# Routing search and proposals with one of each VectorE step's two operands in PSUM

## The chip, the cores and the metric

One core of one Trainium2 chip runs the whole program. The metric is the device time of one execution in microseconds (us); lower is better.

## What is computed

Three layers run one after the other on 4608 tokens of 512 values, all in float32: a retention layer (causal linear attention with a decay per head), a bilinear layer `((x @ w1) * (x @ w2)) @ w3 @ w_out`, and a mixture of eight experts whose tokens are assigned globally. Only the assignment matters here:

```python
cap = N // E                      # 4608 / 8 = 576
logits = x @ w_gate               # 4608 x 8
order = np.argsort(-logits.flatten())
for idx in order:
    tok, e = (int(idx) // E, int(idx) % E)
    if assigned[tok] >= 0 or counts[e] >= cap:
        continue
    assigned[tok] = e
    counts[e] += 1
for e in range(E):
    mask = assigned == e
    h = np.maximum(x[mask] @ w1[e], 0.0)
    out[mask] = h @ w2[e]
```

## The kernel before, in words

The bilinear layer's last product (`y`, 12 blocks of 384 tokens) is only partly done in its own turn. For eight of the blocks it is put off: 24 tiles of 128 tokens, with 24 matmuls each (L893, 576 in all), are left to fill TensorE while the tokens are assigned. These matmuls are called fillers below. For a filler tile ScalarE makes the high part of its input (L888), GpSimd the low part (L889, a tensor_tensor of 128x1024), and ScalarE copies the result out of PSUM (L896); SyncE stores it to `y_scratch`.

The assignment (`route`) is a search for one threshold per expert. It has five rounds and a last check. A round is:

- `propose`: TensorE broadcasts the thresholds `tau` (L694); VectorE masks the logits `LB` below the threshold (L696, L697), takes each token's best expert (`best`, a tensor_reduce at L668), masks what is not the best (L699, L700); TensorE transposes the proposals (L673) and ScalarE copies them to `LP` (L703).
- `search`: VectorE sets up a table of step widths `hs_` (L709, or L711 to L713) and the first trial thresholds (L714). Then come six trips. In a trip VectorE and ScalarE count proposals above three trial thresholds (L716, L717 on VectorE, L719 on ScalarE), a matmul adds the counts up (L676, called the count below), and VectorE compares them with the capacity (L726), moves the trial thresholds (L725 prepares, L728 sets) and `tau` (L729).

Then `place` turns the chosen tokens into a list of token numbers by expert: the running place of each token is compared with the numbers 0 to 127 (`iota`; VectorE, L768 and four times L774), GpSimd multiplies by token numbers (four times L773), 48 small matmuls (L779) collect them, and VectorE writes `idx` (L785). With `idx` GpSimd gathers the rows of the first expert (L977), and the experts' matmuls begin (L1010, L1032).

Every engine works through its own instructions in the order in which they were written down. `merge(route(), lates, LATE)` sets that order here: each `yield` of the routing code names a time, and for it a matching number of fillers is put behind the routing matmul on TensorE's list. So 11 fillers follow a count (in one pair of trips 12 and 10), 5 follow the last count of a round, and 35 stand between the broadcast L694 and the first count of a round (26 in the first round). In the last check 21 stand between L694 and L673. A routing matmul that is late holds up every filler behind it.

`RS` (which holds `tau`, `thr`, `ahead`, `hits`, `r3`), `A2` (`r1`, `r2`, `LP`, `hs_`), `LB` and the constants `C(...)` are in SBUF. `PX[1]` and the two halves `PYb` of the tile `py` are PSUM banks that the attention and the experts use and that stand idle during the routing.

Of the kernel before, what the change touches and what calls it, by code (L numbers as in the profile page):

```python
# [9 lines left out]
AF = mybir.ActivationFunctionType  # L10
OP = mybir.AluOpType
# [5 lines left out]
PT = 96  # L17
# [3 lines left out]
TRIPS = 8  # L21
# [63 lines left out]
def build(ctx, tc, io):  # L85
    nc = tc.nc
    PE, V, A, G, SP = nc.tensor, nc.vector, nc.scalar, nc.gpsimd, nc.sync
# [10 lines left out]
    def C(name):  # L98
        o, n = COFF[name]
        return cst[:, o:o + n]  # L100
# [3 lines left out]
    def region(tag, n, dt):  # L104
        uid[0] += 1
        return sb.tile([128, n], dt, name=f"{tag}_{uid[0]}", tag=tag)
# [6 lines left out]
    A0, A1, A2 = region("a0", 3072, F32), region("a1", 3072, F32), region("a2", 1536, F32)  # L113
# [7 lines left out]
    TR, PX, MM = P[0:2], P[2:4], P[4:6]  # L121
    PY = ps.tile([128, 1024], F32, name="py")
    PYb = [PY[:, 512 * i:512 * i + 512] for i in range(2)]
# [9 lines left out]
    def nxt(name, n):  # L133
        i = rot[name]
        rot[name] = (i + 1) % n
        return i
# [494 lines left out]
    NEG = -1e38  # L631
# [5 lines left out]
    ts_i, ts_f, r3, rt = RS[:PT, 704:800].bitcast(I32), RS[:PT, 800:896], RS[:PT, 896:944], RS[:, 944:1008]  # L637
    r1, r2, LP = A2[:PT, 0:384], A2[:PT, 384:768], A2[:, 768:1056]
    idx = sb.tile([128, 40], I32, name="idx")
    flag = sb.tile([1, 2], I32, name="flag")  # L640
    w0, w0n, tau, wid, hits, off = (rt[:, i:i + 1] for i in range(6))
    thr, ahead, junk = (rt[:, 8 + 3 * i:11 + 3 * i] for i in range(3))
    hs_ = A2[:, 1056:1056 + 6 * TRIPS]
    sc2 = MS[:, 0:288]
    cnt = rh[:, 0:1]

# [7 lines left out]
    def f3(x):  # L654
        return x.rearrange("p (c n) -> p c n", c=3)

    def bcast_j(x):

        return x.rearrange("p (c j) -> p c j", c=3)[:, :, None, :].to_broadcast([PT, 3, 8, 16])

    def f4(x):
        return x.rearrange("p (c e j) -> p c e j", c=3, e=8)

    LBf = LB.rearrange("p c e j -> p (c e j)")

    def best(m):

        V.tensor_reduce(r3.rearrange("p (c j) -> p c j", c=3), m.rearrange("p (c e j) -> p c j e", c=3, e=8),  # L668
                        axis=AX.X, op=OP.max)

    def to_experts(src, out_ps):
        for c in range(3):
            PE.transpose(out_ps[:, PT * c:PT * c + PT], src[:, 128 * c:128 * c + 128], ident[:PT, :PT])  # L673

    def count(out_ps, x):
        PE.matmul(out_ps, blk16, x, start=True, stop=True)  # L676
# [14 lines left out]
    def propose():  # L691

        p = TR[nxt("tr", 2)]
        PE.matmul(p[:PT, :128], tau.to_broadcast([128, PT]), ident, start=True, stop=True)  # L694
        yield 3700
        V.tensor_tensor(f3(r1), f3(LBf), p[:PT, None, :128].to_broadcast([PT, 3, 128]), op=OP.is_lt)  # L696
        V.scalar_tensor_tensor(r1, r1, NEG, LBf, op0=OP.mult, op1=OP.add)  # L697
        best(r1)
        V.tensor_tensor(f4(r2), f4(r1), bcast_j(r3), op=OP.is_lt)  # L699
        V.scalar_tensor_tensor(r1, r2, NEG, r1, op0=OP.mult, op1=OP.add)  # L700
        p = TR[nxt("tr", 2)]
        to_experts(r1, p)
        A.activation(LP, p[:, :288], AF.Copy)  # L703
        yield 2300

    def search(a, trips):

        if a == 0:
            V.tensor_scalar(hs_, C("pw"), w0, 2.0, op0=OP.mult, op1=OP.mult)  # L709
        else:  # L710
            V.tensor_scalar(wid, tau, w0n, 2.0 - 2.0 ** a, op0=OP.is_equal, op1=OP.mult)  # L711
            V.tensor_scalar(wid, wid, 2.0 ** a, w0, op0=OP.add, op1=OP.mult)
            V.tensor_scalar(hs_, C("pw"), wid, None, op0=OP.mult)  # L713
        V.scalar_tensor_tensor(thr, C("sg"), tau, hs_[:, 0:3], op0=OP.mult, op1=OP.add)  # L714
        for i in range(trips):
            V.tensor_scalar(sc, LP, thr[:, 0:1], 0.0, op0=OP.is_ge, op1=OP.add, accum_out=rh[:, 5:6])  # L716
            V.tensor_scalar(sc, LP, thr[:, 1:2], 0.0, op0=OP.is_ge, op1=OP.add, accum_out=rh[:, 6:7])  # L717
            with nc.allow_low_precision(reason="whole numbers up to 288"):
                A.activation(sc2, LP, AF.Sign, bias=thr[:, 2:3], accum_out=rh[:, 7:8])  # L719
            p = TR[nxt("tr", 2)]  # L720
            count(p[:, :3], rh[:, 5:8])
            last = i == trips - 1
            step = hs_[:, 3 * TRIPS + 3 * i:3 * TRIPS + 3 * i + 3]
            if not last:
                V.scalar_tensor_tensor(ahead, C("sg"), tau, hs_[:, 3 * i + 3:3 * i + 6], op0=OP.mult, op1=OP.add)  # L725
            V.scalar_tensor_tensor(junk, p[:, :3], 0.0, C("cap"), op0=OP.add, op1=OP.is_ge, accum_out=hits)  # L726
            if not last:
                V.scalar_tensor_tensor(thr, step, hits, ahead, op0=OP.mult, op1=OP.add)  # L728
            V.scalar_tensor_tensor(tau, step[:, 0:1], hits, tau, op0=OP.mult, op1=OP.add)  # L729
            yield 900 if last else 1900  # L730

    def final_check():
# [13 lines left out]
    def place():  # L746

        V.tensor_tensor_scan(sc, sel, sel, 0.0, op0=OP.add, op1=OP.bypass)
        p = TR[nxt("tr", 2)]
        PE.matmul(p[:, :1], tri16, cnt, start=True, stop=True)  # L750
        yield 1500
        V.tensor_tensor(off, p[:, :1], C("ebase"), op=OP.add)
        V.scalar_tensor_tensor(sc, sc, off, sel, op0=OP.add, op1=OP.mult)
        p = TR[nxt("tr", 2)]
        for c in range(3):
            PE.transpose(p[:PT, 128 * c:128 * c + 128], sc[:, PT * c:PT * c + PT], ident)  # L756
        yield 2000
        V.tensor_reduce(r3.rearrange("p (c j) -> p c j", c=3), p[:PT, :384].rearrange("p (c e j) -> p c j e", c=3, e=8),
                        axis=AX.X, op=OP.max)
        V.tensor_scalar(ts_i[:, 0:48], r3, -1.0, None, op0=OP.add)  # L760
        V.tensor_scalar(ts_i[:, 48:96], ts_i[:, 0:48], 7, None, op0=OP.logical_shift_right)
        V.tensor_scalar(ts_i[:, 0:48], ts_i[:, 0:48], 127, None, op0=OP.bitwise_and)
        V.tensor_copy(ts_f, ts_i)
        pi = PX[0]
        o1, ot = (x[:PT, 3072:4032].bitcast(F16).rearrange("p (n s) -> p n s", s=40) for x in spare[:2])
        lo = gt[NB - 3][:PT].bitcast(F16).rearrange("p (n s) -> p n s", s=128)

        V.tensor_tensor(o1, C("iota")[:PT, None, :40].to_broadcast([PT, 48, 40]),  # L768
                        ts_f[:, 48:96, None].to_broadcast([PT, 48, 40]), op=OP.is_equal)
        yield 2000  # L770
        for a in range(0, 48, 12):
            b = a + 12
            G.tensor_tensor(ot[:, a:b], o1[:, a:b], C("tok")[:PT, a:b, None].to_broadcast([PT, 12, 40]), op=OP.mult)  # L773
            V.tensor_tensor(lo[:, a:b], C("iota")[:PT, None, :].to_broadcast([PT, 12, 128]),  # L774
                            ts_f[:, a:b, None].to_broadcast([PT, 12, 128]), op=OP.is_equal)
            yield 1700
        for ch in range(48):
            g = ch // 16
            PE.matmul(pi[:, 40 * g:40 * g + 40], lo[:, ch], ot[:, ch], start=ch == 0, stop=ch % 16 == 15,  # L779
                      skip_group_check=True)  # L780
        yield 1000
        V.scalar_tensor_tensor(sc[:, 0:120], pi[:, 0:120], 0.5, C("base"), op0=OP.is_gt, op1=OP.mult)
        V.scalar_tensor_tensor(sc[:, 0:120], pi[:, 0:120], 16.0 * PT, sc[:, 0:120], op0=OP.min, op1=OP.add)
        with nc.allow_low_precision(reason="whole numbers up to 4608"):
            V.tensor_reduce(idx, sc[:, 0:120].rearrange("p (g s) -> p s g", g=3), axis=AX.X, op=OP.max)  # L785

    def route():
        for a, steps in ROUNDS:
            yield from propose()
            yield from search(a, steps)  # L790
        yield from final_check()
        good = nc.values_load(flag[:, 0:1], min_val=0, max_val=224)
        with tc.If(good < 224):
            route_exactly()
        yield from place()
# [320 lines left out]
    for c in ORDER.split():  # L1116
        n = int(c[1:])
        if c[0] == "c":
            a, b = (0, 272, 400, CST.shape[1])[n:n + 2]
# [21 lines left out]

    lates = all_late()
    merge(route(), lates, LATE)
    drain(lates)
    drain(weights(0, 0, G))
# [52 lines left out]
```

## Time and profile before

| | us |
|---|---|
| runs | 1332.22, 1334.24, 1333.74 |
| median | 1333.74 |
| the profiled execution | 1332.78 |
| its span, first to last instruction | 1330.8 |

| engine | busy us | share of the span |
|---|---|---|
| TensorE (PE) | 1261.4 | 95% |
| weight loads (PEld) | 1114.0 | 84% |
| VectorE (DVE) | 573.7 | 43% |
| ScalarE (ACT) | 460.2 | 35% |
| GpSimd (POOL) | 262.7 | 20% |

The times of the rows are microseconds from the start of the span. TensorE is busy nearly everywhere; the routing lies between 709 and 882 us. A row of the timeline can stand for several equal instructions in a row (xN); its second number then reaches from the first one's start to the last one's end. A bracket at a row's end says how long the engine was idle before it and what ended that. An instruction on VectorE that is held up after it was issued shows as a longer instruction, not as idle time.

### The profile page before, as it was taken

What the parts mean: (1) busy time and instruction counts of PE and PEld (TensorE: products, weight loads), DVE (VectorE), ACT (ScalarE), POOL (GpSimd) and SP (SyncE); (2) the same over time, 40 slices, a digit from 0 to 9 for tenths busy, and PEclk for the clock granted to TensorE, in tenths of its full rate; (3) what the DMA queues carried; (4) which work ended last, traced back from release to release, by engine and by line L of the source; (5) the groups of instructions that cost most, each with busy time, mean ns of one, the idle gap of its engine ahead of it and who ended that gap; (6) DMA issues with size and microseconds to landing.
All of it is one profiled execution on the core that took longest, in us unless ns stands there. A gap on an engine that the chain in (4) does not pass through costs nothing. (4 is left out here: it accounts for less than half of the span.)

```text
span 1330.8 us, 27168 instructions
## 1 busy us (share of the span) xinstructions
PE 1261.4 (95%) x11406; PEld 1114.0 (84%) x11406; DVE 573.7 (43%) x1298; ACT 460.2 (35%) x987; POOL 262.7 (20%) x238
## 2 busy tenths in 40 slices
PE   5789999999999999999999899869999999999996
PEld 4688988889898998988997676669989989899885
DVE  6796544443232222212215777564524435335220
ACT  4443333343223222222222434234534435335321
POOL 0101111112112020211013533261211202201011
PEclk7799999999999999999999999879999999999999
DMA  8756444422313122242014112044524425334110
GB/s 229 231 168 183 128 136 137 118 75 55 81 23 87 35 66 77 68 127 81 10 48 163 52 40 87 34 155 135 170 69 138 146 84 159 113 118 151 40 45 28
DMA packets 156382, 136.00 MB, mean 102 GB/s; under 512 B 119264, under 2 KB 119520, under 8 KB 155232
## 3 DMA queue, kind: packets, MB, share of 16 engines
q1 hardware_dynamic: 150368, 115.35, 29.4%
q0 software_dynamic: 5888, 18.88, 4.3%
q8 instruction: 91, 1.49, 0.4%
q14 instruction: 35, 0.29, 0.1%
HBM read 107.19 MB, written 27.00 MB: 101 GB/s over the span
## 5 line engine op out<-in xcount | busy, mean ns | idle before, releaser
L549 PE MATMUL p<-x,ws 128*128 128x384 f32 x2304 | 424.1, 339 | 3.1 <-issue 1.6
L549 PEld LDWEIGHTS p<-x,ws 128*128 128x128 f32 x2304 | 398.2, 189 | 11.2 <-issue 4.7
L1032 PE MATMUL p<-ws,g 128*128 128x512 f32 x864 | 218.1, 394 | 1.9 <-DVE rs L1042 1.4
L1032 PEld LDWEIGHTS p<-ws,g 128*128 128x128 f32 x864 | 156.5, 188 | 31.5 <-DVE rs L1042 1.8
L893 PE MATMUL p<-ws,x 128*128 128x512 f32 x576 | 145.5, 406 | 0.0
L558 DVE TENSOR_TENSOR g<-p,ms 128x384 f32<-128x384 f32 x88 | 49.0, 557 | 182.1 <-PE p L549 179.2
L893 PEld LDWEIGHTS p<-ws,x 128*128 128x128 f32 x576 | 107.3, 193 | 20.5
L930 DVE TENSOR_TENSOR ws<-x,ws 128x512 fp32r<-128x512 f32 x120 | 80.7, 690 | 90.6 <-ACT ws L929 82.7
L261 POOL TENSOR_TENSOR a<-a,cst 128x512 f32<-128x512 f32 x52 | 54.6, 1051 | 304.6 <-DMA a<-q 232.3
L345 POOL TENSOR_TENSOR x<-a,x 128x256 fp32r<-128x256 f32 x64 | 49.3, 780 | 257.8 <-ACT x L344 257.8
L929 ACT ACTIVATE ws<-x 128x512 fp32r<-128x512 f32 x128 | 78.1, 628 | 63.4 <-DMA x<-ew 48.4
L556 ACT ACTIVATE ms<-p 128x384 f32<-128x384 f32 x96 | 47.0, 490 | 151.6 <-PE p L549 149.7
L1043 POOL DMA_INDIRECT out<-rs,idx x40 | 40.2, 1006 | 265.4 <-ACT g L1019 146.6
L601 PE MATMUL p<-ws,g 128*128 128x512 f32 x288 | 71.9, 398 | 0.0
L601 PEld LDWEIGHTS p<-ws,g 128*128 128x128 f32 x288 | 52.5, 188 | 13.3 <-issue 2.5
L1010 PE MATMUL p<-a,ws 128*128 128x320 f32 (+1 forms) x384 | 58.9, 303 | 0.5 <-issue 0.5
L1019 ACT ACTIVATE g<-py 128x256 fp32r<-128x256 f32 x96 | 31.5, 328 | 77.9 <-PE py L1010 68.1
L1010 PE MATMUL py<-a,ws 128*128 128x320 f32 (+1 forms) x384 | 57.5, 298 | 0.0
L1010 PEld LDWEIGHTS p<-a,ws 128*128 128x128 f32 x384 | 55.5, 195 | 2.0 <-issue 0.7
L1010 PE MATMUL p<-x,ws 128*128 128x320 f32 (+1 forms) x384 | 56.8, 297 | 0.0
L1010 PEld LDWEIGHTS py<-a,ws 128*128 128x128 f32 x384 | 55.1, 192 | 1.9
L1010 PE MATMUL py<-x,ws 128*128 128x320 f32 (+1 forms) x384 | 56.4, 296 | 0.3 <-DVE g L1020 0.3
(187 smaller groups left out, 1532.7 us busy)
## 6 DMA issues: line engine op xcount, KB each, us to landing
x<-ew SPq DMA_DIRECT2D x128, 256.0 KB, 2.9
y_scratch<-ms SPq DMA_DIRECT2D x36, 256.0 KB, 2.0
a<-k SPq DMA_DIRECT2D x64, 128.0 KB, 3.7
ws<-w SPq DMA_DIRECT2D x8, 1024.0 KB, 10.2
a<-q SPq DMA_DIRECT2D x62, 128.0 KB, 2.9
a<-v SPq DMA_DIRECT2D x31, 256.0 KB, 4.6
g_scratch<-g SPq DMA_DIRECT2D x8, 768.0 KB, 5.5
g<-g_scratch SPq DMA_DIRECT2D x4, 1536.0 KB, 6.7
```

The lines of the kernel that those rows point to most:

```text
L261: (V if t < Q0 else G).tensor_tensor(xx, xx, tb_[:, :, None].to_broadcast([128, H, DH]), op=OP.mult)
L345: G.tensor_tensor(xl.rearrange("p (s a) i -> p s a i", s=2), f, xh.bitcast(F32).rearrange("p (s a) i -> p s a i", s=2), op=OP.subtract)
L549: PE.matmul(p[:, :TB], w[:, kk, fs], x[:, kk, :], start=(kk == 0 and j == 0), stop=(kk == 3 and j == 2))
L556: A.activation(a, p[:, :TB], AF.Copy)
L558: V.tensor_tensor(g[:, f, :], p[:, :TB], a, op=OP.mult)
L601: PE.matmul(p, x[:, f, ts], w[:, f, :], start=(f == 0 and j == 0), stop=(f == 7 and j == 2))
L893: PE.matmul(p, x[:, f, :], w[:, f, :], start=(f == 0 and j == 0), stop=(f == 7 and j == 2))
L929: A.activation(h, st, AF.Copy)
L930: low.tensor_tensor(lo[:, 512 * u:512 * u + 512], st, h.bitcast(F32), op=OP.subtract)
L1010: PE.matmul(p[:, :n], w[:, kk, fs], x[kk][:, ts], start=(kk == 0 and j == 0), stop=(kk == 3 and j == 2))
L1032: PE.matmul(p, x, w[:, f, :], start=(f == 0 and j == 0), stop=(f == 7 and j == len(ops) - 1))
L1043: st = G.indirect_dma_start(out=out, out_offset=bass.IndirectOffsetOnAxis(ap=idx[:n, 5 * e + o:5 * e + o + 1], axis=0), in_=ob[:n], in_off ...
```

## The change

Four tables move into PSUM: the step widths `hs_`, the numbers `iota`, a copy of the logits (`LBp`), and the masked logits (`r1p`). Two ScalarE copies at the start of `route` fill `LBp` and `iota`; VectorE writes `hs_` and `r1p` there itself. Each of the routing's VectorE steps that read two tensors from SBUF (L697, L699, L700, L714, L725, L728, L768, L774) now reads one from PSUM and one from SBUF. The step that moves `tau` (L729) becomes a tensor_scalar: one tensor from PSUM, `hits` and `tau` as scalars per partition.

```diff
-    hs_ = A2[:, 1056:1056 + 6 * TRIPS]
+    hs_, iota = PYb[0][:, 0:6 * TRIPS], PYb[0][:PT, 128:256]
+    LBp, r1p = PYb[1][:PT, 0:384], PX[1][:PT, 0:384]
...
-        V.scalar_tensor_tensor(r1, r1, NEG, LBf, op0=OP.mult, op1=OP.add)
-        best(r1)
-        V.tensor_tensor(f4(r2), f4(r1), bcast_j(r3), op=OP.is_lt)
-        V.scalar_tensor_tensor(r1, r2, NEG, r1, op0=OP.mult, op1=OP.add)
+        V.scalar_tensor_tensor(r1p, r1, NEG, LBp, op0=OP.mult, op1=OP.add)
+        best(r1p)
+        V.tensor_tensor(f4(r2), f4(r1p), bcast_j(r3), op=OP.is_lt)
+        V.scalar_tensor_tensor(r1, r2, NEG, r1p, op0=OP.mult, op1=OP.add)
...
-            V.scalar_tensor_tensor(tau, step[:, 0:1], hits, tau, op0=OP.mult, op1=OP.add)
+            V.tensor_scalar(tau, step[:, 0:1], hits, tau, op0=OP.mult, op1=OP.add)
...
-        V.tensor_tensor(o1, C("iota")[:PT, None, :40].to_broadcast([PT, 48, 40]),
+        V.tensor_tensor(o1, iota[:, None, :40].to_broadcast([PT, 48, 40]),
...
-            V.tensor_tensor(lo[:, a:b], C("iota")[:PT, None, :].to_broadcast([PT, 12, 128]),
+            V.tensor_tensor(lo[:, a:b], iota[:, None, :].to_broadcast([PT, 12, 128]),
...
     def route():
+        A.activation(LBp, LBf, AF.Copy)
+        A.activation(iota, C("iota")[:PT], AF.Copy)
```

The lists of the engines stay as they were but for the following. The line numbers of the changed kernel are one higher from L644 on (L696 became L697), and three higher behind the two new lines of `route` (L888 became L891).

VectorE at the start of the second round, before (`rs` holds the thresholds and scalars, `a` the proposals and, before, the step widths, `p` and `py` are PSUM, `cst` the constants):

```order
L729 SCALAR_TENSOR_TENSOR rs_76<-a_11_74,rs_76 128x1
L711 TENSOR_SCALAR rs_76<-rs_76 128x1
L712 TENSOR_SCALAR rs_76<-rs_76 128x1
L713 TENSOR_SCALAR a_11_74<-cst,rs_76 128x48
L714 SCALAR_TENSOR_TENSOR rs_76<-cst,rs_76,a_11_74 128x3
L725 SCALAR_TENSOR_TENSOR rs_76<-cst,rs_76,a_11_74 128x3
L696 TENSOR_TENSOR a_11_74<-LB,p_82 96x384
L697 SCALAR_TENSOR_TENSOR a_11_74<-a_11_74,LB 96x384
L668 TENSOR_REDUCE rs_76<-a_11_74 96x48
L699 TENSOR_TENSOR a_11_74<-a_11_74,rs_76 96x384
L700 SCALAR_TENSOR_TENSOR a_11_74<-a_11_74 96x384
```

and the same place in the changed kernel:

```order
L730 TENSOR_SCALAR rs_76<-py,rs_76 128x1
L712 TENSOR_SCALAR rs_76<-rs_76 128x1
L713 TENSOR_SCALAR rs_76<-rs_76 128x1
L697 TENSOR_TENSOR a_11_74<-LB,p_82 96x384
L698 SCALAR_TENSOR_TENSOR p_85<-a_11_74,py 96x384
L669 TENSOR_REDUCE rs_76<-p_85 96x48
L714 TENSOR_SCALAR py<-cst,rs_76 128x48
L700 TENSOR_TENSOR a_11_74<-p_85,rs_76 96x384
L715 SCALAR_TENSOR_TENSOR rs_76<-cst,rs_76,py 128x3
L701 SCALAR_TENSOR_TENSOR a_11_74<-a_11_74,p_85 96x384
L726 SCALAR_TENSOR_TENSOR rs_76<-cst,rs_76,py 128x3
```

The three steps that set up the widths and the first trial thresholds stood ahead of the proposal's five steps; they now stand between these. It is so in all five rounds.

ScalarE ahead of the first round, before:

```order
L585 ACTIVATE rs_76<-p_87 128x384
L888 ACTIVATE x_7_70<-g_22_5785 128x1024
L703 ACTIVATE a_11_74<-p_83 128x288
L896 ACTIVATE ms_75<-p_86 128x512
L719 ACTIVATE ms_75,rh<-a_11_74,rs_76 128x288 x2
```

and changed:

```order
L585 ACTIVATE rs_76<-p_87 128x384
L789 ACTIVATE py<-LB 96x384
L790 ACTIVATE py<-cst 96x128
L891 ACTIVATE x_7_70<-g_22_5785 128x1024
L704 ACTIVATE a_11_74<-p_83 128x288
L899 ACTIVATE ms_75<-p_86 128x512
L720 ACTIVATE ms_75,rh<-a_11_74,rs_76 128x288 x2
```

The two copies stand behind the last logits' copy and ahead of the first filler tile's input. On TensorE the first round's L673 moves two fillers back (16 instead of 14 stand ahead of it, 10 instead of 12 behind it); all else there, and all on GpSimd and SyncE, stands as before.

## Rows read from the trace of the kernel before

**Rows 1.** Who waited for whom, TensorE, 705 to 882 us: total, times, longest.

```profile
PE p L676 <- DVE rs L717: 11.9, 12, 2.2
```

**Rows 2.** Timeline of VectorE and GpSimd: start, length, engine, line, operation, output and inputs.

```profile
741.29 0.54 DVE L696 TENSOR_TENSOR a<-LB,p 96x384 f32<-96x384 f32 x1
741.39 2.39 POOL L889 TENSOR_TENSOR x<-g,x 128x1024 fp32r<-128x1024 f32 x1 [1.28 <-ACT x L888]
...
761.19 2.39 POOL L889 TENSOR_TENSOR x<-g,x 128x1024 fp32r<-128x1024 f32 x1 [3.67 <-ACT x L888]
...
761.61 0.16 DVE L726 SCALAR_TENSOR_TENSOR rs<-p,cst 128x3 f32<-128x3 f32 x1 [1.03 <-PE p L676]
...
761.88 1.72 DVE L728 SCALAR_TENSOR_TENSOR rs<-a,rs 128x3 f32<-128x3 f32 x1
```

**Rows 3.** Four routing lines on VectorE: shortest/median/longest in ns, first and last start.

```profile
L728 DVE SCALAR_TENSOR_TENSOR rs<-a,rs x25: 221/1121/2396, 720.1 to 839.5; 128x3 f32<-128x3 f32 x25
...
L716 DVE TENSOR_SCALAR_CACHE_REDUCE rs<-a,rs x30: 499/504/515, 717.9 to 841.9; 128x288 f32<-128x288 f32 x30
...
L726 DVE SCALAR_TENSOR_TENSOR rs<-p,cst x30: 161/164/165, 719.8 to 843.3; 128x3 f32<-128x3 f32 x30
...
L700 DVE SCALAR_TENSOR_TENSOR a<-a x6: 553/554/2635, 715.8 to 847.4; 96x384 f32<-96x384 f32 x6
```

**Rows 4.** Timeline of TensorE: broadcasts (L694), counts (L676) and transposes (L673) of the rounds.

```profile
712.80 0.38 PE L694 MATMUL p<-cst,rs 128*96 128x128 f32 x2
...
758.73 0.18 PE L676 MATMUL p<-rh,blk 128*128 128x3 f16 x1
...
761.38 0.18 PE L676 MATMUL p<-rh,blk 128*128 128x3 f16 x1
...
764.78 0.18 PE L676 MATMUL p<-rh,blk 128*128 128x3 f16 x1 [0.60 <-DVE rs L717]
...
790.89 0.18 PE L676 MATMUL p<-rh,blk 128*128 128x3 f16 x1 [0.82 <-DVE rs L717]
...
792.17 0.38 PE L694 MATMUL p<-cst,rs 128*96 128x128 f32 x2
...
797.70 0.47 PE L673 MATMUL p<-cst,a 96*128 96x96 f32 x3
...
801.03 0.18 PE L676 MATMUL p<-rh,blk 128*128 128x3 f16 x1
...
844.33 0.38 PE L694 MATMUL p<-cst,rs 128*96 128x128 f32 x2
...
850.07 0.47 PE L673 MATMUL p<-cst,a 96*128 96x96 f32 x3 [0.57 <-DVE a L700]
```

**Rows 5.** Timeline of ScalarE ahead of the first round.

```profile
716.50 1.06 ACT L888 ACTIVATE x<-g 128x1024 fp32r<-128x1024 f32 x1 [6.22 <-PE p L893]
```

**Rows 6.** The token lists, 859 to 882 us: timeline, lines with ns, and the store's landing.

```profile
859.20 3.76 PE L893 MATMUL p<-ws,x 128*128 128x512 f32 x8
...
865.12 2.15 DVE L768 TENSOR_TENSOR ws<-cst,rs 96x1920 f16<-96x1920 f32 x1
...
875.57 0.78 PE L779 MATMUL p<-ws,g 96*128 96x40 f16 x24
...
879.45 0.46 PE L779 MATMUL p<-ws,g 96*128 96x40 f16 x12 [2.01 <-POOL ws L773]
...
876.44 0.32 SPq L898 DMA_DIRECT2D y_scratch<-ms  x1
...
881.16 1.32 POOL L977 DMA_INDIRECT a<-y_scratch,idx  x1 [1.76 <-DMA x<-ew]
...
L774 DVE TENSOR_TENSOR g<-cst,rs x4: 2541/2542/3950, 867.2 to 876.0; 96x1536 f16<-96x1536 f32 x4
...
L773 POOL TENSOR_TENSOR ws<-ws,cst x4: 2500/2504/2506, 869.5 to 876.9; 96x480 f16<-96x480 f16 x4
...
DMA to landing us min/median/max: 2.0/2.0/2.0
```

## The prediction, made before the changed kernel ran

> **What bounds the kernel now.** TensorE is busy for 95% of the span, so the first view to read is who it waits for in the routing. One line carries most: the counts wait 11.9 us, in 12 trips, for VectorE's L717 [rows 1]. That is what shows as idle time; held fillers show only as a longer way from one count to the next. The second view is the timeline of VectorE beside GpSimd. At 761.19 GpSimd starts the low part of a filler tile, 2.39 us long. Inside it VectorE's L726, with one operand in PSUM, takes its usual 0.16. The next step, L728, reads two tensors of three numbers each from SBUF and takes 1.72, until GpSimd's step is over [rows 2]. The lines of VectorE say that this is the rule here: L728 takes 0.22 at best, 1.12 in the median and 2.40 at worst, which is the length of GpSimd's step; L726 takes 0.161 to 0.165 in all 30 cases; L716, with one tensor and one scalar from SBUF, never exceeds 0.515 [rows 3]. And at 741.29 a step with LB in SBUF and its second operand in PSUM lets GpSimd start 0.10 behind it and keep its 2.39 [rows 2]. So in this trace two SBUF tensors wait for GpSimd, one doesn't.
>
> What that costs TensorE is read from the third view, the counts. From 758.73 to 761.38 a trip takes 2.65: eleven fillers and the count, 0.24 each, and nothing waits. The next, with the held L728, takes 3.40 and ends in a wait of 0.60 [rows 4]. Had L728 taken 0.22, VectorE's side of that trip would have been 3.40 - 1.50 = 1.90, well below the 2.65 of the fillers. So the fillers are the floor of a trip, and what a trip takes above 2.65 is the price of the hold.
>
> **The change part by part.**
>
> *Trips and proposals.* From the first round's broadcast at 712.80 to the last check's at 844.33 the five rounds take 131.53 [rows 4]. A round without holds: 22 fillers from L694 to L673, 22 x 0.24 = 5.28; from L673 to the first count 3.33 (797.70 to 801.03, no wait shown); five trips of 2.65, 13.25; from the last count to the next broadcast 1.28 (790.89 to 792.17) [rows 4]. Together 23.14. The first round has 26 instead of 35 fillers ahead of its first count: 9 x 0.24 = 2.16 less, 20.98. Four times 23.14 and 20.98 make 113.54; the gain is 131.53 - 113.54 = 18.0.
>
> *The last check's proposal.* It takes 844.33 to 850.07, 5.74, with L673 waiting 0.57 for L700, which was held once (2.635 instead of 0.554) [rows 3, 4]. With 21 fillers its floor is 5.04: a gain of 0.7. The same rows give VectorE's side of a proposal without holds: 5.74 - 2.08 = 3.66.
>
> *What moves into the proposals.* The three steps for widths and thresholds now stand between the proposal's five, two of them ahead of L700. Small steps take about 0.22 (the shortest L728 [rows 3]), so with the gaps some 0.5 is added: 3.66 + 0.5 = 4.16. In rounds two to five 5.28 of fillers cover that. In the first round only 16 fillers stand there, 3.84, and 0.3 is lost. If the cover were gone altogether the price would be 5 x 0.5 = 2.5.
>
> *PSUM as an operand.* No row shows VectorE writing PSUM. Reading it costs 0.164 in L726 against 0.221 in the shortest L728, the same shape [rows 3]: bounds of -0.06 and, taking the same for a loss, +0.06 a step. I take nothing, since up to 0.75 a trip is covered by fillers. [...]
>
> *The two ScalarE copies.* ScalarE idles for 6.22 ahead of 716.50 [rows 5], the copies are smaller than the 128x1024 that takes 1.06 there, and their first reader comes a step behind the first broadcast. Nothing; 0.1 in the first round at most, with ScalarE's order there, makes the first round's loss 0.4 together.
>
> *The token lists.* L774 and L773 take turns: both read 2.5 us each, four of each, and the last 12 small matmuls wait 2.01 for L773 and start at 879.45 [rows 6]. L768, 1920 elements, took 2.15 before GpSimd's step was free, so 1536 elements alone are 2.15 x 0.8 = 1.72 [rows 6]. Four L774 from 867.2 end at 874.1. L773 alone has no row: 0.8 is what is left of 2.5 beside 1.72, 2.5 is the other end; I take 1.1, the pace of GpSimd's 1024 elements in 2.39 for 480 [rows 2]. Behind the last low part, near 868.3, four end at 872.8. Both are then done before TensorE leaves the fillers at 875.57, and the last 12 small matmuls start three steps of 0.39 later, at 876.7. The gather follows 1.71 behind (879.45 to 881.16), at 878.5. It also needs the last rows of `y`: issued at 876.44, landed 2.0 later, 878.4, with some 0.3 to GpSimd's start 878.7 [rows 6]. That store becomes what is late. Gain 881.16 - 878.7 = 2.4; with L773 at 2.5 alone it would be 1.1. Behind the gather the expert's start hangs on it in the same way as now.
>
> **Sum:** 18.0 + 0.7 - 0.4 + 2.4 = 20.7. The profiled execution took 1332.78, so 1312.1; it lies 0.96 below the median of the runs, 1333.74, which makes the forecast **1313.0**.
>
> **The rivals.**
>
> *ScalarE becomes the bound.* A trip also needs ScalarE's third count (L719), which stands behind the two steps of a filler tile, L888 (1.06 [rows 5]) and the copy of half that size, some 1.6 together. With VectorE unheld, a pair that stands just ahead of a sign could end up to 1.6 - 0.75 = 0.85 late. About a dozen pairs stand between two counts; at 0.5 each that is 6, a gain of 14.7 and 1319. Against it: the trip up to 761.38 has such a pair right behind its sign and shows none. Chance 0.10.
>
> *The token lists give nothing back:* L773 is slow by itself, or the expert's first weights or the slower fillers there decide. 1315.4. I count it into the forecast's own range.
>
> *The hold does not go with the operand's memory.* It could hang on the scalars per partition, `hits` and `tau`, which stay in SBUF: L726 and L696, the steps that pass, have none. Then all holds stay, and the three steps that now stand inside the proposals lengthen what TensorE waits for by 0.5 in each of five rounds: 1333.7 + 2.5 = 1336.2, slower. It decides if L728's median stays above 1 us. Against it: L716 has such a scalar and passes 30 times [rows 3]. Chance 0.03 for this; 0.02 that part of the holds goes and part of the price comes, within 0.2% of before.
>
> *Something in between:* a hold that stays on one of the steps, 1316 to 1325. Chance 0.05.
>
> **How the numbers follow.** The forecast has 0.80. Its own range: behind the branch eight fillers took 3.76, 0.47 each instead of 0.24 [rows 6]; if TensorE stalls less they may run at full pace, 1.9 less there and as much again at the experts' start, and the first round may lose nothing: 1309. Without the lists' gain and with half of ScalarE's price it is 1319. So 1309 to 1319, which leaves out some 2 in 10: the rest of ScalarE's case, the in-between case and the two without gain. A measurement of this kernel can tell about 0.2%, 2.7 us, from no change. Faster by more: 0.80 + 0.10 + 0.05 = 0.95; within: 0.02; slower: 0.03.
>
> **What would show it.** After: L728's longest near 0.25 and GpSimd's low part still 2.39; counts 2.65 apart in all rounds, and no wait of L676 for L717; 113 to 115 us from the first broadcast to the last check's; L774 near 1.7 and the gather right behind the landing of the last `y`. The prediction is wrong if a step with one operand in PSUM is still as long as GpSimd's, if ScalarE's L719 releases the counts, or if the gain of the rounds is given back at the experts' start.

## The result, and the profile after

The changed kernel takes 1312.4 us in the median of four runs (1310.5 to 1313.4), beside 1333.4 for the kernel before on the same chip: a ratio of 0.9841, 95% interval 0.9824 to 0.9859. The forecast was 1313.0, range 1309 to 1319. The profiled execution took 1313.27, with a span of 1311.2; before it was 1330.8, so the traces differ by 19.6.

The first line of the page of after gives busy times and shares of the span.

```profile
PE 1257.6 (96%) x11406; PEld 1114.9 (85%) x11406; DVE 530.5 (40%) x1298; ACT 461.0 (35%) x989; POOL 253.8 (19%) x238
```

VectorE's busy time falls by 43 us with the same count of steps; TensorE's falls by 4. The waits of TensorE in the routing and the lists (705 to 882 us: total, times, longest) are now these, all of them. The 11.9 us for VectorE's L717 of [rows 1] are gone; the 3.9 at L751 is TensorE's own sequencer at the branch, which was 3.6 before.

```profile
PE p L991 <- DMA a<-y_scratch,idx: 7.8, 2, 6.1
PE p L751 <- PEq L796: 3.9, 1, 3.9
PE p L1013 <- ACT a L996: 0.5, 1, 0.5
PE p L677 <- ACT ms L720: 0.4, 1, 0.4
```

The lines of VectorE (shortest/median/longest in ns) answer to [rows 3]. L729 is the old L728, L717 the old L716, L727 the old L726, L701 the old L700; L698, L669 and L730 are the masking step that now writes PSUM, the reduce that reads it, and the step that moves `tau`.

```profile
L729 DVE SCALAR_TENSOR_TENSOR rs<-py,rs x25: 220/221/223, 722.2 to 825.6; 128x3 f32<-128x3 f32 x25
...
L717 DVE TENSOR_SCALAR_CACHE_REDUCE rs<-a,rs x30: 501/505/513, 720.3 to 826.0; 128x288 f32<-128x288 f32 x30
...
L727 DVE SCALAR_TENSOR_TENSOR rs<-p,cst x30: 161/163/164, 721.9 to 828.0; 128x3 f32<-128x3 f32 x30
...
L701 DVE SCALAR_TENSOR_TENSOR a<-a,p x6: 542/543/549, 718.1 to 831.8; 96x384 f32<-96x384 f32 x6
...
L698 DVE SCALAR_TENSOR_TENSOR p<-a,py x6: 557/557/559, 716.3 to 830.1; 96x384 f32<-96x384 f32 x6
...
L669 DVE TENSOR_REDUCE rs<-p x6: 553/553/553, 716.8 to 830.7; 96x48 f32<-96x384 f32 x6
...
L730 DVE TENSOR_SCALAR rs<-py,rs x30: 267/270/279, 722.3 to 828.2; 128x1 f32<-128x1 f32 x30
```

The longest step that moves the trial thresholds went from 2.396 (the old L728) to 0.223 (L729), and none of these lines has a tail any more. Two steps of `place` with two SBUF tensors were left as they were, the scan L748 and the scalar_tensor_tensor L753 (here L749 and L754); no GpSimd step runs beside them in this trace, and they take 0.759 and 0.519 as before. So not every step of the routing with two SBUF tensors has changed; v1 below shows what that can cost. The timeline of GpSimd, VectorE and TensorE in the third round shows the same meeting as [rows 2], with the other end: GpSimd's low part starts at 774.08, L729 runs through inside it in 0.22, and the counts (L677) stay 2.65 apart, 768.48 to 781.71 in five trips.

```profile
768.48 0.18 PE L677 MATMUL p<-rh,blk 128*128 128x3 f16 x1
...
774.08 2.42 POOL L892 TENSOR_TENSOR x<-a,x 128x1024 fp32r<-128x1024 f32 x1 [3.40 <-ACT x L891]
...
774.28 0.22 DVE L729 SCALAR_TENSOR_TENSOR rs<-py,rs 128x3 f32<-128x3 f32 x1
...
781.71 0.18 PE L677 MATMUL p<-rh,blk 128*128 128x3 f16 x1
```

Behind the search the timeline of TensorE, SyncE's queue and GpSimd answers to [rows 4, 6]:

```profile
829.06 0.38 PE L695 MATMUL p<-cst,rs 128*96 128x128 f32 x2
...
834.08 0.41 PE L674 MATMUL p<-cst,a 96*128 96x96 f32 x3
...
843.48 0.16 PE L751 MATMUL p<-rh,tri 128*128 128x1 f16 x1 [3.91 <-PEq L796]
...
849.87 10.49 SPq L901 DMA_DIRECT2D y_scratch<-ms  x3
...
859.17 1.39 PE L780 MATMUL p<-ws,g 96*128 96x40 f16 x48
...
861.23 0.29 DVE L786 TENSOR_REDUCE idx<-rs 128x40 int32<-128x120 f32 x1
...
863.00 1.15 POOL L980 DMA_INDIRECT a<-y_scratch,idx  x1 [7.37 <-DMA x<-ew]
```

With the first broadcast at 715.17, these give the account of the 19.6:

| stretch of the span, us | before | after | gain |
|---|---|---|---|
| start to the first broadcast | 712.80 | 715.17 | -2.4 |
| five rounds, first broadcast to last | 131.53 | 113.89 | 17.6 |
| last check's proposal, to the transpose | 5.74 | 5.02 | 0.7 |
| transpose to L750 (L751 after) | 9.11 | 9.40 | -0.3 |
| from there to the first gather | 21.98 | 19.52 | 2.5 |
| first gather to the end | 449.6 | 448.2 | 1.4 |

The first row and the last are not put down to the change. A second trace of the changed kernel (below) has the first broadcast at 713.68 and 451.5 behind the gather, and in the eleven traces of the experiments the first broadcast lies anywhere from 710.0 to 716.4, on kernels of either kind.

### The profile page after: what moved, and what is told of

It is laid out like the page before. It is cut to its first block, busy times and chain, and to the rows that moved or that the text cites. A ratio compares the mean times of both kernels' runs of the same rounds, so it can differ in the third digit from the quotient of the medians.

```text
span 1311.2 us, 27175 instructions
## 1 busy us (share of the span) xinstructions
PE 1257.6 (96%) x11406; PEld 1114.9 (85%) x11406; DVE 530.5 (40%) x1298; ACT 461.0 (35%) x989; POOL 253.8 (19%) x238
## 5 line engine op out<-in xcount | busy, mean ns | idle before, releaser
L896 PE MATMUL p<-ws,x 128*128 128x512 f32 x576 | 141.8, 401 | 0.0
L896 PEld LDWEIGHTS p<-ws,x 128*128 128x128 f32 x576 | 105.7, 190 | 20.7 <-issue 0.4
L933 DVE TENSOR_TENSOR ws<-x,ws 128x512 fp32r<-128x512 f32 x120 | 80.9, 690 | 96.9 <-ACT ws L932 96.7
```

The source lines that it names most:

```text
L896: PE.matmul(p, x[:, f, :], w[:, f, :], start=(f == 0 and j == 0), stop=(f == 7 and j == 2))
L933: low.tensor_tensor(lo[:, 512 * u:512 * u + 512], st, h.bitcast(F32), op=OP.subtract)
```

## The experiments

The theory: a VectorE step with two tensors in SBUF waits while GpSimd's low part runs (L728 up to 2.396 us [rows 3]), and the rest follows from that. Against it stand the rivals that the proposals or the lists carry the gain, that a step with a PSUM operand is simply cheaper, that the hold goes with something else than the operand's memory, and that GpSimd has nothing to do with it. Each run was compared with the kernel before on the same chip. The times that were expected were reckoned from 1333.7; where the kernel before took less on the run's chip, it is the gain that answers to the expectation.

### The three parts one by one

**x1_search:** the kernel before, with

```diff
-    hs_ = A2[:, 1056:1056 + 6 * TRIPS]
+    hs_ = PYb[0][:, 0:6 * TRIPS]
-            V.scalar_tensor_tensor(tau, step[:, 0:1], hits, tau, op0=OP.mult, op1=OP.add)
+            V.tensor_scalar(tau, step[:, 0:1], hits, tau, op0=OP.mult, op1=OP.add)
```

> The kernel before with only the step widths hs_ in PSUM, and L729 as a tensor_scalar; the proposals and the token lists stay with two SBUF tensors. Theory (a VectorE step with two SBUF tensors waits for GpSimd, and the trips carry the gain): before, the trips of the five rounds stood 16.1 us above their floor of 2.65 a trip, the proposals 1.9 in the rounds and 0.7 in the last check, the lists 2.4. So L728 at 0.25 at most, no wait of L676 for L717, and a gain of 13 to 17 us: 1317 to 1321. Rival A, the gain lies in the proposals: a gain under 5 us, above 1328. Rival B, with L728 released the hold only moves on to the proposals' steps (L697, L699, L700), which now come at other times: L728 short, but a gain of 5 to 12, 1322 to 1329.

1316.6, beside 1331.6: 0.9892 (0.9876 to 0.9909), 15.0 us. The five rounds take 116.58, 14.95 less than before. Two of VectorE's lines, and one of TensorE's waits:

```profile
L728 DVE SCALAR_TENSOR_TENSOR rs<-py,rs x25: 220/221/223, 718.0 to 823.9; 128x3 f32<-128x3 f32 x25
...
L699 DVE TENSOR_TENSOR a<-a,rs x6: 553/1966/2606, 713.2 to 829.8; 96x384 f32<-96x384 f32 x6
```

```profile
PE p L673 <- DVE a L700: 2.2, 3, 1.3
```

L728 is free as in the changed kernel, with `hits` and `tau` still in SBUF as scalars. The proposals' L699, left with two SBUF tensors, is still held, up to 2.61, and TensorE waits 2.2 for L700. So most of the gain is the trips', and the hold moves on without costing much: the gain lies in the 13 to 17 that were expected, not in rival B's 5 to 12.

**x2_proposals:** the kernel before, with

```diff
+    LBp, r1p = PYb[1][:PT, 0:384], PX[1][:PT, 0:384]
-        V.scalar_tensor_tensor(r1, r1, NEG, LBf, op0=OP.mult, op1=OP.add)
-        best(r1)
-        V.tensor_tensor(f4(r2), f4(r1), bcast_j(r3), op=OP.is_lt)
-        V.scalar_tensor_tensor(r1, r2, NEG, r1, op0=OP.mult, op1=OP.add)
+        V.scalar_tensor_tensor(r1p, r1, NEG, LBp, op0=OP.mult, op1=OP.add)
+        best(r1p)
+        V.tensor_tensor(f4(r2), f4(r1p), bcast_j(r3), op=OP.is_lt)
+        V.scalar_tensor_tensor(r1, r2, NEG, r1p, op0=OP.mult, op1=OP.add)
+        A.activation(LBp, LBf, AF.Copy)
```

> The kernel before with only the proposals changed: the masked logits r1p and the copy LBp of the logits in PSUM; the trips and the lists stay with two SBUF tensors. Theory: L699, L700 and L697 stay near 0.55, L728 is held as before (median about 1.1), and the gain is 1 to 4 us: 1330 to 1333. Rival A, the gain lies in the proposals: over 10 us, below 1324. Rival B, the hold does not go with the operand's memory: one of the three steps still reaches over 2 us, and the time is 1333 to 1335.

1328.0, beside 1331.6: 0.9975 (0.9965 to 0.9984), 3.6 us. In its trace the rounds give 2.15 (129.38). The hold has left the steps that changed, and those alone (L729 is here the old L728 and L700 the old L699); the counts still wait 12.0 us for VectorE:

```profile
L729 DVE SCALAR_TENSOR_TENSOR rs<-a,rs x25: 221/1230/2396, 717.0 to 834.5; 128x3 f32<-128x3 f32 x25
...
L700 DVE TENSOR_TENSOR a<-p,rs x6: 553/553/553, 712.3 to 841.6; 96x384 f32<-96x384 f32 x6
```

**x3_lists:** the kernel before, with

```diff
+    iota = PYb[0][:PT, 128:256]
-        V.tensor_tensor(o1, C("iota")[:PT, None, :40].to_broadcast([PT, 48, 40]),
+        V.tensor_tensor(o1, iota[:, None, :40].to_broadcast([PT, 48, 40]),
-            V.tensor_tensor(lo[:, a:b], C("iota")[:PT, None, :].to_broadcast([PT, 12, 128]),
+            V.tensor_tensor(lo[:, a:b], iota[:, None, :].to_broadcast([PT, 12, 128]),
+        A.activation(iota, C("iota")[:PT], AF.Copy)
```

> The kernel before with only the numbers iota in PSUM, so that the token lists' L768 and L774 have one operand there. Theory: L774 falls from 2.54 to about 1.7 and L773 from 2.50 to 1.0, as they did in the changed kernel, the rounds stay as before, and the gain is 2.4 us, 1331.3 (1.1 to 2.5, as the last store of y allows). Rival, the lists give nothing back, because the experts' first weights or the last y decide the start: within 0.5 of before, 1333 to 1334. The three single parts should add up to the whole change's 21 us, within about 2.

1330.4, beside 1331.6: 0.9992 (0.9976 to 1.0008). The time alone doesn't tell it from nothing; the trace does, here by the lines of the two list steps and the timeline behind them.

```profile
L775 DVE TENSOR_TENSOR g<-py,rs x4: 1744/1744/1744, 864.4 to 869.4; 96x1536 f16<-96x1536 f32 x4
...
L774 POOL TENSOR_TENSOR ws<-ws,cst x4: 1001/1002/1003, 865.7 to 868.5; 96x480 f16<-96x480 f16 x4
```

```profile
873.27 1.39 PE L780 MATMUL p<-ws,g 96*128 96x40 f16 x48
...
877.12 1.15 POOL L979 DMA_INDIRECT a<-y_scratch,idx  x1 [7.61 <-DMA x<-ew]
```

The two no longer take turns at 2.5 us, and from the small matmuls' first to the gather it takes 3.85 instead of 5.59 [rows 6]: 1.7 us. The rounds, where this kernel changes nothing on VectorE, came out 1.4 shorter than in the trace of before, all of it in the first round (25.97 instead of 27.38; the other four take 104.20 and 104.14). By that much the price of held steps can differ between two traces without a change on VectorE's side.

The medians of the three give 15.0 + 3.6 + 1.2 = 19.8, beside 18.1 to 21.0 for the whole change in two comparisons. Within the spread of the medians the parts add up.

### GpSimd's work taken away

**y1_before_nolow**, and **y2_after_nolow** on the changed kernel:

```diff
+    n_low = [0]
-        G.tensor_tensor(gl, g, gh.bitcast(F32), op=OP.subtract)
+        if n_low[0] < 2:
+            G.tensor_tensor(gl, g, gh.bitcast(F32), op=OP.subtract)
+        n_low[0] += 1
```

> The kernel before with no operand moved; GpSimd makes the low part (L889) for the first two filler tiles only, so the low parts of the other 22 tiles are left out. Theory (the hold is GpSimd's work, not something that PSUM gives by itself): L728 at 0.25 at most, the counts 2.65 apart, a gain in the rounds like the change's, 17 to 19 us, and the lists still taking turns with L773, so 1314 to 1317. Rival (steps with a PSUM operand are simply cheaper, or the moved order does it): L728 stays near 1.1 in the median and the time within 3 us of before.

> The changed kernel with GpSimd's low part (L892) made for the first two filler tiles only; the low parts of the other 22 tiles are left out. Theory (the change took away the whole price of the hold): nothing more is to be had in the rounds, first broadcast to last 113.9 within 0.3, and the time is 1312 within 2. Rival (part of the hold is left somewhere, as a slower step that shows no wait): 3 us or more below the changed kernel, under 1309.

y1: 1313.2, beside 1331.6: 0.9862 (0.9846 to 0.9879), 18.4 us. No operand has moved, and yet two of VectorE's lines and TensorE's wait for it read:

```profile
L728 DVE SCALAR_TENSOR_TENSOR rs<-a,rs x25: 221/224/1095, 718.5 to 823.7; 128x3 f32<-128x3 f32 x25
...
L699 DVE TENSOR_TENSOR a<-a,rs x6: 553/554/555, 713.7 to 829.5; 96x384 f32<-96x384 f32 x6
```

```profile
PE p L676 <- DVE rs L717: 2.1, 2, 1.9
```

The two waits that are left, and the 1.095, lie in the first round (723.59 and 728.26), where GpSimd makes other low parts, those of the first expert's weights (L930, in this kernel L933, 128x512, 1.29 each), which this kernel keeps: the same hold from another line. Rounds two to five take 92.24, and 92.18 in the changed kernel. So the gain is the release from GpSimd's step; the rival that PSUM operands are cheaper falls. y2: 1312.2, beside 1332.1: 0.9845 (0.983 to 0.986), rounds 113.47 beside 113.89; the 0.4 between them lies in the first round (21.33 and 21.71). Nothing of the hold is left in the changed kernel's rounds.

The trace of y1 also shows where "one SBUF tensor doesn't wait" ends. L713, a tensor_scalar that reads one tensor from SBUF and writes SBUF, takes 0.247 to 0.249 elsewhere; here it lasts until GpSimd's step is over (timeline of GpSimd and VectorE; the first row is two steps):

```profile
732.99 2.54 POOL L933 TENSOR_TENSOR ws<-x,ws 128x512 fp32r<-128x512 f32 x2
...
734.83 0.74 DVE L713 TENSOR_SCALAR a<-cst,rs 128x48 f32<-128x48 f32 x1
```

In y5 below it takes 0.724 in the same way; these two are the only times in the thirteen traces that it starts inside a GpSimd step that outlasts it. Where it writes `hs_` to PSUM instead, it starts inside one 12 times and is never held (0.257 to 0.258 in the trace of after). The counting steps (L716, L717) and the 128x1 steps (L711, L712) read one SBUF tensor too and are not held: in the trace of after 28 of the counting steps start inside a GpSimd step that outlasts them and take 0.500 to 0.514, and one 128x1 step does and takes 0.216. So what sets L713 apart stays open.

### GpSimd's work increased

**y3_before_more** and **y4_after_more:** one more GpSimd step behind each low part in the code, on either kernel, with `more` a piece of `A2` that nobody reads.

```diff
+    more = A2[:, 1104:1504].rearrange("p (f t) -> p f t", f=8)
         G.tensor_tensor(gl, g, gh.bitcast(F32), op=OP.subtract)
+        G.tensor_tensor(more, g[:, :, 0:50], g[:, :, 64:114], op=OP.subtract)
```

> The kernel before with one more GpSimd step of 128x400 behind each low part (L889), an estimate of 0.95 us from L889's 2.39 for 1024 elements; its output is not used. Theory: 24 x 0.95 = 23 us more of GpSimd time during the routing hold more of VectorE's steps; the 24 low parts (57 us) cost about 18, so by proportion 7 us more (3 to 10): 1335 to 1342, with L728's longest above 2.4. Rival (GpSimd's steps hold VectorE only for another reason, such as a wait of their own that they share with ScalarE's L888): within 1 of before.

> The changed kernel with the same additional GpSimd step of 128x400 behind each low part. Theory: with one operand of each step in PSUM VectorE no longer sees GpSimd: 113.9 from first to last broadcast as without it, and the time within 1 of the changed kernel, 1311 to 1314. Rival (the change only shortened the steps and the hold still acts): 2 us or more above it.

Both expectations missed: y3 1333.2, beside 1332.1 (1.0006, 0.9997 to 1.0016); y4 1317.2, beside 1332.1 (0.9893, 0.9874 to 0.9912), 4.8 above the changed kernel's 1312.4. These are the numbers of the two rivals, but neither run tests them. The timeline of GpSimd in y3 tells why:

```profile
713.77 3.32 POOL L891 TENSOR_TENSOR a<-a 128x400 f32<-128x400 f32 x3
```

The additional step reads only the tile's raw input, and on GpSimd's list it came not behind each low part but three at a time and far ahead of it: nine before the routing, twelve between 713 and 732, three at 815. The experiment had not put its work where the search is. In y4 it makes the first round's low parts late: TensorE waits 1.9 for GpSimd at 728.09, then 1.0 for ScalarE ahead of the last count at 734.71, with a granted clock of 0.74 between the two. The first round takes 25.98 instead of 21.71, which is 4.3 of the 4.8. Its other four rounds take 92.18, as without the additional work.

**y5_before_behind** and **y6_after_behind:** the same, but the additional step reads the low part, and so stands behind it.

```diff
-        G.tensor_tensor(more, g[:, :, 0:50], g[:, :, 64:114], op=OP.subtract)
+        G.tensor_tensor(more, gl[:, :, 0:50].bitcast(F32), gl[:, :, 64:114].bitcast(F32), op=OP.subtract)
```

> As y3, but the additional GpSimd step of 128x400 now reads the low part itself, so that it stands right behind each L889 on GpSimd's list; in y3 most of them had run ahead of the routing or in its first round, in groups of three (1.06 each). Theory, as y3's rows bear it out: a VectorE step that waits is let in when GpSimd's step ends, and the next one with two SBUF tensors waits for the next GpSimd step. So behind a held L728 (2.40 at most, as before) L729 is now held by the additional step, up to 1.06 longer (1.3), and the sign with it: about 20 low parts in the rounds, most of them in trips that had run out of slack, 10 to 18 us: 1342 to 1350. Rival (GpSimd does not hold VectorE, and y3's 1 us is the whole price): 1332 to 1335.

> As y4, but with the additional step behind each low part, as in y5; y4 lost its 4.3 us in the first round alone, where TensorE waited 1.9 for a low part that GpSimd's grouped additional steps had made late. Theory: no VectorE step is held; first broadcast to last 113.9 to 115, the time 1312 to 1315. Rival (the hold acts on the changed kernel too): 1320 or more.

y5: 1341.5, beside 1330.5: 1.0074 (1.0052 to 1.0096), 11 us slower. y6: 1312.3: 0.986 (0.9839 to 0.9881), the time of the changed kernel (1312.4 in the same comparison). So the same work costs 11 us with two SBUF operands and nothing beyond the noise with one in PSUM. In the trace of y6 the rounds take 114.94; what is above 113.89 lies in the first round, whose last count waits 1.6 for ScalarE's L720, and L729 stays at 0.220 to 0.223. The time of y5 lies just under its range, the 11 near the low end of the 10 to 18 expected. In its rounds the additional step costs 6.6 (138.11 instead of 131.53), and 1.7 between L756 and the gather, where it delays the lists; the other 2.6 of its trace stand ahead of the first broadcast, where executions differ by as much without it. The timeline of VectorE and GpSimd in y5 shows why it isn't more:

```profile
761.50 1.06 POOL L891 TENSOR_TENSOR a<-x 128x400 f32<-128x400 f32 x1
...
761.93 0.65 DVE L725 SCALAR_TENSOR_TENSOR rs<-cst,rs,a 128x3 f32<-128x3 f32 x1
...
766.23 1.73 DVE L728 SCALAR_TENSOR_TENSOR rs<-a,rs 128x3 f32<-128x3 f32 x1
...
767.87 0.21 DVE L729 SCALAR_TENSOR_TENSOR rs<-a,rs 128x1 f32<-128x1 f32 x1
...
768.01 1.05 POOL L891 TENSOR_TENSOR a<-x 128x400 f32<-128x400 f32 x1
...
772.96 2.12 DVE L699 TENSOR_TENSOR a<-a,rs 96x384 f32<-96x384 f32 x1
...
774.74 1.25 POOL L891 TENSOR_TENSOR a<-x 128x400 f32<-128x400 f32 x1
...
775.11 1.30 DVE L700 SCALAR_TENSOR_TENSOR a<-a 96x384 f32<-96x384 f32 x1
```

L729, expected to be the next step held, starts 0.14 ahead of the additional step here and passes; in rounds two to five all 24 take 0.20 to 0.22. What the additional step holds in the trips is L725, twice a round, 0.63 to 0.65 instead of 0.22. In the proposals one step after the other is held, L699 by the low part and L700 by the additional step. The trips of the five rounds became 3.0 longer and the proposals 3.5.

### The changed kernel again, and a version beyond it

**z_change_again** is the changed kernel once more, for a second trace.

> The changed kernel once more, beside the other two on one chip, for a second trace: whether the stretch at half clock at 124 to 131 us, which its first trace has and the trace of before has not, belongs to the change (then it is there again and the first broadcast comes near 715) or to the execution (then the first broadcast comes anywhere from 710 to 715, as in the other kernels). The time 1311 to 1314.

1312.4, beside 1330.5: 0.9856 (0.9835 to 0.9876). The first broadcast comes at 713.68, the rounds take 113.78, L751 to the gather 19.52. The windows of 123 to 132 us (length, busy time and instructions of PE, PEld, DVE, ACT and POOL, granted clock, DMA share, GB/s) show what differs ahead of the routing; first the first trace of after, then z:

```profile
123.00:132.00 9.00, 7.61 (x130) 6.99 (x130) 0.16 (x1) 1.58 (x3) 2.78 (x3) 0.62 0.47 115
```

```profile
123.00:132.00 9.00, 7.19 (x135) 6.99 (x134) 1.51 (x4) 2.54 (x6) 4.56 (x6) 0.83 0.59 147
```

The granted clock is 0.62 and 0.83 there; it is 1.00 in the trace of before, but also in that of y4, which holds the change, and 0.62 in that of y3, which does not. So the stretch below 1.00 (a granted 0.50 from 125 to 130 us in the first trace of after) comes and goes with the execution, on kernels of either kind. It shows in five of the six traces that hold the whole change and in two of the seven others; whether the change makes it likelier stays open.

**v1_fill** is the changed kernel with fillers moved from behind L757 to where TensorE idles ahead of L751, by the two `yield`s at the end of the final check and at the start of `place`:

```diff
         V.tensor_copy(flag[:, 0:1], p[:1, :1])
-        yield 1000
+        yield 4300
...
         PE.matmul(p[:, :1], tri16, cnt, start=True, stop=True)
-        yield 1500
+        yield 900
```

> The changed kernel with about 12 of the 52 fillers that stand behind L757 put in front of the branch, where TensorE idles for 3.9 us ahead of L751; nothing else moves. What limits the lists now is VectorE's last L775 and the landing of the last y. Theory: the fillers run in the idle time, the last y and the lists' matmuls come earlier by 2 to 3 us, and with them the gather: 1309.5, 1309 to 1311. Rival (the gather is held by the lists on VectorE, which the fillers do not move): within 0.7 of the changed kernel, or slower if L751 now waits for fillers: 1312 to 1314.

1308.0 (1307.5 to 1308.7), beside 1332.1: 0.9814 (0.9801 to 0.9828), 4.4 below the changed kernel's 1312.4 (from another comparison) and beyond its expected range. Ahead of L751 23 fillers now stand instead of 4, behind L757 36 instead of 52, and between the two 5 instead of 8: more were moved than the twelve meant (timeline of TensorE, GpSimd and VectorE):

```profile
837.05 5.51 PE L896 MATMUL p<-ws,x 128*128 128x512 f32 x23
...
841.98 2.38 POOL L892 TENSOR_TENSOR x<-ws,x 128x1024 fp32r<-128x1024 f32 x1 [3.54 <-ACT x L891]
...
842.71 0.16 PE L751 MATMUL p<-rh,tri 128*128 128x1 f16 x1 [0.15 <-PEq L796]
...
843.10 1.57 DVE L754 SCALAR_TENSOR_TENSOR rs<-rs 128x288 f32<-128x288 f32 x1
...
845.02 8.46 PE L896 MATMUL p<-ws,x 128*128 128x512 f32 x36
...
857.38 1.14 POOL L980 DMA_INDIRECT a<-y_scratch,idx  x1 [4.51 <-DMA x<-ew]
```

From L742 to the gather it takes 20.45 instead of 24.74: 4.3. The idle time gives 3.76 of that (0.15 instead of 3.91). Another 1.4 goes with the clock: from L742 to the small matmuls TensorE is busy for 15.6 instead of 17.0, with the same 64 fillers. In the changed kernel the eight fillers behind the idle time run at a granted 0.58 (first row); with the idle time filled the clock stays at 1.00 throughout, as the windows of v1 from L742 to the small matmuls say (the other rows; length, PE's busy time and instructions, granted clock, DMA share, GB/s):

```profile
843.48:846.66 3.18, 3.18 (x9) 0.58 0.02 5
```

```profile
836.93:842.71 5.78, 5.63 (x27) 1.00 0.14 51
842.71:844.73 2.02, 1.41 (x6) 1.00 0.36 131
844.73:853.32 8.59, 8.59 (x40) 1.00 0.09 34
```

Some 0.8 is lost again. L754, one of the two steps that the change left with two SBUF tensors, now meets a low part and takes 1.573 instead of 0.519; L757 waits 0.61 for it. And what limits the gather now is `idx` on VectorE: TensorE's last 12 small matmuls wait 1.19 for L775, and from the first small matmul to the gather it takes 4.06 instead of 3.83. That L754 with one operand in PSUM would bring the gather forward by about as much as it is held is an estimate from these rows; no run tried it.

## Why the prediction was right, point by point

**Who holds whom.** Right. It was read from three lines of the trace of before [rows 2, 3], and y1, y2, y5 and y6 show it from both sides: without GpSimd's step no hold, with more of it more price, and with one operand in PSUM none either way. Over all thirteen traces, between 705 and 885 us, 136 VectorE steps with two tensors in SBUF start inside a GpSimd step that outlasts them, and all 136 are held; of 423 with one of the two in PSUM none is. For the same three numbers (L728, and L729 of after) that is up to 2.40 against 0.22. The prediction's "one doesn't" holds for the steps that it named, and not for L713, which y1 and y5 caught. The rival in which the scalars per partition hold the step has fallen: all 25 L729 of after take `hits` from SBUF and stay at 0.220 to 0.223.

**The rounds.** The sum was 113.54 and 0.4 for the first round, 113.94; measured 113.89 and 113.78. Rounds two to five take 23.03 to 23.08 where 23.14 was reckoned. The first takes 21.71 where 20.98 and 0.4, 21.38, was, and not for the reason that was reckoned. L674 comes 0.26 later than before, but it stands two fillers further back; the first count comes 6.48 behind the broadcast (6.74 before), where the prediction's own terms without a loss give 6.45. So the 0.4 of the small steps and the copies was not lost. The excess lies in two trips instead, one of 2.88, for which no wait shows, and the last of 3.19, the one trip that ScalarE ends (the 0.4 of L720 in the waits). That is the rival of a dozen such pairs, cut down to one. That the total came within 0.05 is in part luck: four rounds 0.1 shorter each, one 0.3 longer.

**The last check's proposal.** 5.02 measured, 5.04 reckoned.

**What moved into the proposals.** The three small steps cost TensorE nothing in rounds two to five: no wait of L674 for L701 is left. The 5.28 of fillers cover them, as the prediction named.

**PSUM as an operand.** Taken as nothing, within 0.06: right, but the comparison behind the 0.06 was not one of memories. L726 has no scalar per partition and L728 has one, `hits`. In the changed kernel both have one tensor in PSUM, and they stay as far apart, 0.163 (L727) and 0.221 (L729). The 3 numbers of L729 take 0.221 with an operand in PSUM and 0.221 in the shortest L728 before; L701 0.543 where L700 took 0.554; L698, which writes PSUM, 0.557 where the old L697 took 0.554 unheld. The reduce gains: 0.553 from PSUM where L668 took 0.829 from SBUF:

```profile
L668 DVE TENSOR_REDUCE rs<-a x6: 812/829/837, 714.4 to 845.9; 96x48 f32<-96x384 f32 x6
```

L730 became dearer, 0.270 instead of 0.213. It now has two scalars per partition instead of one, and the step above from no scalar to one is 0.058; but its tensor also moved into PSUM, and no run parts the two. Fillers cover it.

**The token lists.** The mechanism held, two sizes were off and cancelled. L775 takes 1.744 (1.72 reckoned) and L774 0.992 (1.1 taken between 0.8 and 2.5), as the rows of x3 show nearly alike; the small matmuls run without a wait, and the last `y` is what the gather waits for. But the step "landed 2.0 later, with some 0.3 to GpSimd's start" was mis-sized. The last `y` store's issue, 0.32 long, ends at 860.36 in the trace of after (849.87 + 10.49), and the gather starts 2.64 behind that, 2.96 behind its start; in all seven traces where this store decides (after, x3, y1, y2, y4, y6, z) it is 2.64 to 2.66. So it took 3.83 from the first small matmul to the gather, not 3.13, and this part gave 1.76 and not 2.4. The missing 0.7 came from the fillers behind the branch, 15.69 from L751 to the small matmuls instead of 16.39, at a granted clock of 0.58 instead of 0.50 for the first 3 us and 0.97 instead of 0.95 behind. The experiments other than v1 took anywhere from 15.7 to 17.0 there, on kernels of either kind, so that gain is not the change's to keep, and that the lists came out at 2.5 was luck. What fills the microsecond between landing and gather stays open.

**The sum.** 20.7 reckoned for the profiled execution, 19.5 measured (1332.78 to 1313.27). Rounds, check and lists with their fillers gave 20.8; -0.3 ahead of L751, -2.4 ahead of the routing and 1.4 behind the gather make up the rest, and the last two differ between executions as well: by 1.5 and 3.3 between the two traces of the changed kernel alone.

## What to carry to other kernels

Where a small VectorE step has a duration that ranges up to exactly that of a GpSimd step, compare it with its neighbours by the memory of their operands; here moving one of two SBUF tensors into an idle PSUM bank took the hold away (the longest from 2.396 to 0.223) without a step more in the loop, and the scalars per partition stayed in SBUF. Go through all steps with two SBUF tensors, also those that no GpSimd step meets yet: L754 took 0.519 until v1 moved the fillers, and 1.573 then. Price it by the floor of the loop (here the fillers between two counts), not by the sum of the held time: the 25 L728 together became 21.5 us shorter (27.0 to 5.5), and the rounds of x1 gave 15. Of an experiment that adds work to a queue, look up where on the engine's list it stands: y3 and y4 measured another place than the one meant.

## What the runs showed that was not expected

- The hold works in both directions: GpSimd's list step takes 0.992 beside VectorE steps with one operand in PSUM and 2.50 while it takes turns with those with two in SBUF [rows 6].
- VectorE's reduce of 96x384 to 96x48 reads faster from PSUM, 0.553, than from SBUF, 0.829.
- The indirect gather starts 2.96 behind the start of the issue of the store whose rows it reads, though that store has landed after 2.0 [rows 6]; where `idx` decides, it starts 0.29 behind `idx` (857.38 in v1).
- The idle time of TensorE ahead of L751 (3.91 in the trace of after) cost more than itself: in twelve traces the fillers between L750 and L756 (L751 and L757), right behind it, ran at a granted 0.50 to 0.72, and at 1.00 in v1, where the idle time was filled (0.50 is the trace of before, 0.58 that of after). In v1 that is worth 1.4 beside the 3.76 of the idle time.
